# First mixture layer of a three-part kernel: its two projections fused per feature tile, against all features first with the gated product kept in DRAM

## The chip, the cores and the metric

The kernel runs on one core of one Trainium2 chip. The metric is the device time of one execution in microseconds (us), as the median of several runs. The engines are TensorE (PE for its matmuls, PEld for its weight loads), VectorE (DVE), ScalarE (ACT), GpSimd (POOL) and SyncE (SP), which issues every DMA here. PSUM has eight banks of 128 x 512 fp32, which matmuls write and DVE and ACT read.

## The reference

```python
q_s = softmax(q, over d);  k_s = softmax(k, over the sequence)      # 4 batches, 8 heads, 576 tokens, 64
attn = q_s @ (k_s^T @ v)                                            # linear attention
x = attn as 2304 tokens x 512
x = ((x @ w_a) * (x @ w_b)) @ w_out                                 # first layer: 512 -> 1536 -> 512
h = x @ w_in                                                        # second layer: 512 -> 2048
P = a0 + a1*h + a2*h^2 + a3*h^3
Q = 1 + |b0|*|h| + |b1|*h^2
out = (P / (Q + 1e-6)) @ w_out2                                     # 2048 -> 512
```

All five weight matrices reach the kernel as 64-bit floats. Each is turned into fp32 by integer arithmetic on the chip, and then, like every operand of a large matmul, parted into a high and a low part (hi + lo). A product of two such operands is three matmuls: hi x hi, hi x lo, lo x hi.

## The kernel before

Tokens lie along the free dimension. There are five token blocks: four wide ones of 512 and a narrow one of 256 (block 4). The first layer has 12 feature tiles of 128, and the hidden size 512 is four slices of 128. For one feature tile and one wide block, the input projection is 2 x 4 x 3 = 24 matmuls of 128x512 (`w_a` and `w_b`, four slices, three passes), and the output projection is 4 x 3 = 12.

Attention comes first: 16 units (batch, pair of heads), four to a batch. A unit loads kx, q, v (the last four also k), takes softmaxes on DVE, ACT and POOL, transposes on PE, and writes its slice of x into `XH` and `XL`. Token block 0 needs batch 0, block 1 needs batches 0 and 1, block 2 needs 1 and 2, blocks 3 and 4 need batch 3.

The first layer is fused per feature tile. For a feature tile f and a block n, `front` (or `raw_p`) projects into two banks, ACT copies the one, DVE multiplies the two in PSUM, and ACT and DVE part the product h into hi and lo in SBUF. Then its output projection is summed over some tiles in four banks and added to `ACC`, which holds the first layer's output in SBUF, four slices of 512 columns to a wide block:

- Tiles 0 to 2: `step1`, plain, for the blocks 0, 1, 2, 4, 3 in this order, between the attention units.
- Tiles 3 to 8, in three pairs, for two wide blocks at a time: the input projection is plain (`raw_p`), and the output projection is done by seven products in place of eight (`seven`, lines 604 to 640), a 2 x 2 block scheme after Strassen and Winograd with feature tiles on the one side and blocks on the other. The sums of h are made on DVE and POOL, the sums of the weights (`combined`) on POOL. A product is 3 matmuls here, twice (q = 0, 1): 2 x 7 x 3 = 42 matmuls where the plain form has 48. Block 4 is plain (`narrow_out`).
- Tiles 9 to 11: plain again (`step1`, and `late_jobs` for block 3).

Within one run of `seven` four banks are chained: bank bb starts as ACT's copy of bank ba, and DVE twice reads bb, adds s5 and writes another bank before PE may add the next product to bb.

Meanwhile the second layer's weights are converted, summed for its own seven-product scheme, parted and sent to DRAM (`spill_in` to `wi`, `spill_out` to `wo`). The second layer (`slot`, `value`, `jobs`) loads them back. Its input projection is by seven products for two feature tiles and two wide blocks, `value` computes the quotient P/Q on ACT, DVE and POOL, and `jobs` does the output projection.

The order on every engine is set by a list planner (class `Plan`). Each operation has an engine, an estimated duration and a rank. At every step the operation that can start earliest by the estimates is placed, and the rank breaks ties; the ranks come from the step number and from the table `K`. The result is one fixed order per engine, kept in the program. PE's gaps in the first 34 us of that plan are filled with 64 x 64 matmuls (line 1029) that compute nothing. DVE operations marked `port` and all POOL operations are planned so that they do not run at once.

Of the kernel before, what the change touches and what calls it, by code (L numbers as in the profile page):

```python
# [8 lines left out]
F32 = mybir.dt.float32  # L9
# [5 lines left out]
U32 = mybir.dt.uint32  # L15
# [15 lines left out]
class Plan:  # L31
# [4 lines left out]
    FILL_NS, FILL_MAX = 220, (99, 10)  # L36
    FILL_BEFORE, FILL_AFTER = 34000, 2000000
# [7 lines left out]
    def add(self, eng, ns, rank, fn, reads=(), writes=(), lat=0, port=False, kind=None):  # L45
# [13 lines left out]
        self.ops.append((eng, ns, rank, fn, deps, lat, port, kind))  # L59

    def run(self, fill=None):
# [15 lines left out]
        held, last = 0.0, None  # L77
        while any(pending.values()):
# [27 lines left out]
        for i in order:  # L106
            fill(-1 - i) if i < 0 else self.ops[i][3]()
# [3 lines left out]
def tile_kernel(ctx: ExitStack, tc: tile.TileContext, q, k, kx, v, w_a, w_b, w_out, w_in, w_out2, ca, cb, out):  # L111
# [23 lines left out]
    MID = [0, 1, 4, 2, 3]
    SC = 672
    HALF = W // 2
    OP = 2 * HALF
    SLOT = 2.5
    TURN1, NX, SW0, SW1, OP1 = 4, 2, 2, 3, NF2 // 2 - 1  # L140
    FREE, SEED = (4, 5, 6), (2, 3, 7)
    K = dict(late=-5.492, soon=-4.219, asoon=-10.236, wl=0.745, j0=0.985, j1=2.536, jn=-5.433, each=0.116, by=0.067, v1=1.075, v2=1.344, v3=2.483, v4=-0.278, v5=1.767, p1=0.009, px=-33.016, op=35.311, w2=-24.837, w2f=35.283, o0=-6.141, o1=0.018, l0=2.085, l1=1.554, l2=-8.695, l3=44.833, last=0.124, wd0=-177.696, wd1=-244.762, wd2=786.423, wd3=-216.948, wd4=-330.707, wd5=-371.667, wd6=-374.53, wd7=-318.414, wd8=945.62, wd9=-244.134, ud0=-407.821, ud1=-374.884, ud2=-251.536, ud3=774.452, ud4=866.463, ud5=897.008, ud6=902.77, ud7=-216.823, ud8=846.88, ud9=-177.926, ud10=868.092, ud11=818.136, ud12=-251.038, ud13=846.209, ud14=808.362, ud15=-311.04, wr0=-371.708, wr1=866.784, wr2=799.828, wr3=-388.518, wr4=858.306, wr5=-269.879, wr6=751.328, wr7=-450.468, wr8=887.219, wr9=846.842, ur0=-250.344, ur1=796.637, ur2=945.186, ur3=901.846, ur4=-216.266, ur5=723.759, ur6=856.445, ur7=-375.494, ur8=-270.336, ur9=709.668, ur10=-383.977, ur11=-376.01, ur12=-338.73, ur13=-335.107, ur14=945.651, ur15=-268.887, nx=7.017, wn=-21.267, sp=-2.053, se=2115.662, msoon=-6.362, madd=-62.481, mcomb=-16.671, mn=-103.581, mpe=0.747, mpb=0.526, mfr=-9.292, mw=-39.037)
# [14 lines left out]
    diag = const.tile([P, P], F32, name="diag")  # L157
    NW4 = NT // W * W
    SIDE = 16
    XH = const.tile([P, NCC, NW4], F32R, name="XH")  # L160
    XL = const.tile([P, NCC, NW4], F32R, name="XL")
    XN = const.tile([P, 8 * SIDE + 2 * NCC * (NT - NW4)], F32R, name="XN")

    def X(low, c, o, n):

        if o < NW4:
            assert o + n <= NW4
            return (XL if low else XH)[:, c, o:o + n]
        i = SIDE + (low * NCC + c) * (NT - NW4) + o - NW4
        return XN[:, i:i + n]  # L170

    def pieces(o, n):
        c = min(max(NW4 - o, 0), n)
        return [(a, b) for a, b in ((0, c), (c, n)) if b > a]

    ACC = const.tile([P, NCC * NT], F32, name="ACC")
    ps = [psum.tile([P, W], F32, name=f"ps{i}") for i in range(8)]
    Y, AB, AT = (0, 1, 2, 3), (4, 5), (6, 7)


# [13 lines left out]
    wa = Area((NW + NHL + NEW) * 2 * W, F32R, "wa")  # L194
    o_sc = NRAW * 2 * W
    o_g = o_sc + NSC * SC
    o_sg = o_g + 2 * W
    o_x = o_sg + 2 * W
    fa = Area(o_x + 2 * W, F32, "fa")

    small = tiles(2, [P, 8 * C5 + 3], F32, "small")
    mxs = tiles(2, [P, 1], F32, "mx")

    two = "p (a b) -> p a b"
    pair = lambda got: [(t.rearrange(two, a=2), k) for t, k in got]
# [18 lines left out]
    def pe(passes, n, rank, fn, reads, writes, fixed=3):  # L224
        plan.add("pe", passes * (n / 2.4 + fixed), rank, fn, reads, writes, kind="r" if passes == 3 else "f")
# [10 lines left out]
    def dve2(n, rank, fn, reads, writes):  # L236
        plan.add("dve", 65 + n * 0.85, rank, fn, reads, writes, port=True)
# [10 lines left out]
    def xk(name, c, o, n):  # L248
        return [(name, c, i) for i in range(o // 32, (o + n - 1) // 32 + 1)]
# [836 lines left out]
```

## Time and profile before

| | |
|---|---|
| median of 3 runs | 887.16 us (886.65 to 887.49) |
| profiled execution, from its first to its last instruction (span) | 885.0 us |
| what lies around the span, by the median | 2.16 us |
| TensorE busy | 875.9 us, 99% |
| weight loads busy | 727.4 us, 82% |
| DVE, ACT, POOL busy | 665.0, 572.6, 448.0 us |
| granted TensorE clock | 1.00, which is 2.4 GHz, over the whole span |
| DMA | 131.25 MB, 148 GB/s over the span |

The profile states no time of the profiled execution besides its span, so the span stands for it, and 2.16 us is added to get from spans to medians. A busy share near 100% on PE means that PE hardly ever waited. It does not say that each matmul ran at its peak, since consecutive matmuls overlap: their listed durations add up to more than the time between their starts. Times of PE work are therefore read from starts. The stages by the timeline: up to 24 us PE has only the attention's small matmuls; from 24 to about 140 us attention and first layer are mixed; the first layer alone runs until about 500 us, and the second until the end.

### The profile page before, as it was taken

To read this page: it belongs to the slowest core of one execution; us is meant where nothing else is said; L and a number is where in the kernel's file an instruction comes from. 1 tells how busy PE (TensorE), PEld (TensorE's weight loads), DVE (VectorE), ACT (ScalarE), POOL (GpSimd) and SP (SyncE) were. 2 spreads that over 40 slices of the span, in tenths; PEclk is the share of its full clock that TensorE was granted. 3 is DMA by queue.
4 is the path that set the end of the run, shared out by engine and by line. 5 is a ranking of instruction groups with operands and counts; after the bars stand their busy time and mean duration, and the time that the engine had idled before them with its cause. 6 is when DMAs were issued, how large, how long until landed. Compare 5 with 4: busy or idle time off the path is not lost.

```text
span 885.0 us, 13244 instructions
## 1 busy us (share of the span) xinstructions
PE 875.9 (99%) x4526; PEld 727.4 (82%) x4526; DVE 665.0 (75%) x1117; ACT 572.6 (65%) x1078; POOL 448.0 (51%) x421
## 2 busy tenths in 40 slices
PE   8999999999999999999999999999999999999998
PEld 7777778888888878888898888888888888888887
DVE  6887766657677675878665698779898878788883
ACT  6877566455455454454534598888888778887770
POOL 4654665355353545362536345455667644455541
PEclk9999999999999999999999999999999999999999
DMA  7866966524414343264542843352525364435222
GB/s 253 271 208 187 279 192 207 182 96 134 153 49 136 114 131 96 72 214 143 179 131 84 248 126 115 112 168 82 175 72 178 107 201 144 158 93 190 69 87 96
DMA packets 60180, 131.25 MB, mean 148 GB/s; under 512 B 6480, under 2 KB 14928, under 8 KB 60112
## 3 DMA queue, kind: packets, MB, share of 16 engines
q1 hardware_dynamic: 60112, 130.40, 46.1%
q8 instruction: 36, 0.59, 0.3%
q14 instruction: 32, 0.26, 0.1%
HBM read 100.49 MB, written 29.88 MB: 147 GB/s over the span
## 4 chain that ended last, share of the span: by engine, by line
PE 97%; DVE 1%; DMA 1%; ACT 0%; POOL 0%; issue 0%; SPq 0%; DVEq 0%; POOLq 0%
PE ps L522 23%; PE ps L524 22%; PE ps L523 22%; PE ps L800 6%; PE ps L802 6%; PE ps L801 6%; PE ps L622 2%; PE ps L624 2%; PE ps L623 2%; PE ps L499 2%; PE ps L464 1%; PE ps L489 1%; PE ps L442 1%; PE ps L1029 1%; DMA wa<-wo 1%; DMA ACC<-in_q 0%
## 5 line engine op out<-in xcount | busy, mean ns | idle before, releaser
L522 PE MATMUL ps<-wa 128*128 128x512 f32 (+1 forms) x428 | 163.2, 381 | 0.8 <-DMA wa<-wo 0.7
L524 PE MATMUL ps<-wa 128*128 128x512 f32 (+1 forms) x428 | 160.8, 376 | 0.0
L523 PE MATMUL ps<-wa 128*128 128x512 f32 (+1 forms) x428 | 160.7, 375 | 0.0
L522 PE MATMUL ps<-XH,wa 128*128 128x512 f32 x384 | 154.3, 402 | 0.0
L759 POOL TENSOR_TENSOR fa<-fa 128x512 f32<-128x512 f32 x72 | 93.4, 1300 | 115.8 <-ACT fa L757 99.5
L524 PE MATMUL ps<-XH,wa 128*128 128x512 f32 x384 | 150.0, 391 | 0.0
L523 PE MATMUL ps<-XL,wa 128*128 128x512 f32 x384 | 149.8, 390 | 0.0
L783 POOL TENSOR_TENSOR wa<-fa,wa 128x512 fp32r<-128x512 f32 x70 | 89.7, 1297 | 41.1 <-ACT wa L782 22.6
L540 DVE TENSOR_TENSOR ACC<-ps,ACC 128x512 f32<-128x512 f32 (+1 forms) x121 | 80.5, 679 | 31.3 <-PE ps L524 25.7
L522 PEld LDWEIGHTS ps<-wa 128*128 128x128 f32 x428 | 80.4, 188 | 17.4 <-DMA wa<-wo 1.1
L524 PEld LDWEIGHTS ps<-wa 128*128 128x128 f32 x428 | 80.4, 188 | 14.8
L523 PEld LDWEIGHTS ps<-wa 128*128 128x128 f32 x428 | 80.5, 188 | 14.4
L800 PE MATMUL ps<-XH,wa 128*128 128x512 f32 x224 | 87.3, 390 | 0.0
L802 PE MATMUL ps<-XH,wa 128*128 128x512 f32 x224 | 87.3, 390 | 0.0
L801 PE MATMUL ps<-XL,wa 128*128 128x512 f32 x224 | 87.2, 389 | 0.0
L524 PEld LDWEIGHTS ps<-XH,wa 128*128 128x128 f32 x384 | 72.1, 188 | 15.6
L522 PEld LDWEIGHTS ps<-XH,wa 128*128 128x128 f32 x384 | 72.2, 188 | 14.7
L523 PEld LDWEIGHTS ps<-XL,wa 128*128 128x128 f32 x384 | 72.2, 188 | 13.7
L349 POOL TENSOR_TENSOR fa<-fa 128x256 fp32r<-128x256 f32 x64 | 49.9, 794 | 55.9 <-ACT fa L348 44.0
L321 POOL TENSOR_TENSOR wa<-fa,wa 128x512 fp32r<-128x512 f32 x30 | 40.1, 1339 | 70.9 <-ACT wa L320 68.7
L766 DVE SCALAR_TENSOR_TENSOR fa<-fa,coef,ps 128x512 f32<-128x512 f32 x72 | 52.7, 741 | 16.2 <-ACT ps L765 15.9
L756 ACT ACTIVATE fa<-ps 128x512 f32<-128x512 f32 x72 | 42.5, 595 | 24.3 <-PE ps L802 11.0
(130 smaller groups left out, 1993.1 us busy)
## 6 DMA issues: line engine op xcount, KB each, us to landing
wa<-wi SPq DMA_DIRECT2D x120, 256.0 KB, 3.0
wa<-wo SPq DMA_DIRECT2D x32, 512.0 KB, 4.7
fa<-in_moe_w_out SPq DMA_DIRECT2D x28, 512.0 KB, 4.4
wi<-fa SPq DMA_DIRECT2D x40, 256.0 KB, 2.5
fa<-in_moe_w_in SPq DMA_DIRECT2D x16, 512.0 KB, 4.2
fa<-in_moe_w_b SPq DMA_DIRECT2D x12, 512.0 KB, 4.0
fa<-in_moe_w_a SPq DMA_DIRECT2D x12, 512.0 KB, 4.1
wi<-wa SPq DMA_DIRECT2D x24, 256.0 KB, 4.9
```

The costliest lines, as they stand in the source:

```text
L349: pool(HALF, rank, lambda: nc.gpsimd.tensor_tensor(out=lo, in0=src, in1=hi.bitcast(F32), op=ALU.subtract), [ksrc, kt], [kt])
L522: nc.tensor.matmul(o, lh, rh, start=start, stop=False)
L523: nc.tensor.matmul(o, lh, rl, start=False, stop=False)
L524: nc.tensor.matmul(o, ll, rh, start=False, stop=stop)
L540: dve(n, rank, lambda: nc.vector.tensor_tensor(out=a, in0=ps[bank][:, :n], in1=a, op=ALU.add), [psk(bank), ("accr", o)], [("accr", o)])
L756: act(n, rank, lambda: A.activation(u, h, AF.Abs), [kh], [ku])
L759: pool(n, rank, lambda: G.tensor_tensor(out=w, in0=w, in1=u, op=ALU.mult), [ku, kw], [kw])
L766: dve(n, rank, lambda: V.scalar_tensor_tensor(out=z, in0=z, scalar=coef[:, 0:1], in1=h, op0=ALU.add, op1=ALU.mult), [kz, kh], [kz], ptr=1)
L783: pool(W, rank, lambda: nc.gpsimd.tensor_tensor(out=hl[1], in0=z, in1=hl[0].bitcast(F32), op=ALU.subtract), [kz, kh], [kh])
L800: T.matmul(ps[bank], wh, xh, start=first, stop=False, skip_group_check=True)
L801: T.matmul(ps[bank], wh, xl, start=False, stop=False, skip_group_check=True)
L802: T.matmul(ps[bank], wl, xh, start=False, stop=last, skip_group_check=True)
```

## The change

The first layer is no longer fused. All 12 feature tiles are projected first, h goes to DRAM as fp32, and the output projection is a pass of its own.

- Tiles 0 to 2 are projected plainly (`plain`), tiles 3 to 11 by seven products (`strassen`) for the block pairs (0, 1) and (2, 3), with `w_a` and `w_b` of a tile as the two rows of the scheme and the two halves of the hidden size as its columns. Block 4 stays plain. One `strassen` is 7 x 2 x 3 = 42 matmuls for what took 48. The two block pairs use four banks each in turn.
- The sums of x that the scheme needs are made once for each block pair (`factors`), the sums of the weights for each tile (`product_weights`).
- `product` copies one bank on ACT, multiplies on DVE into SBUF, and `stored` sends the 128 x 512 fp32 result to DRAM (`h_d`, 60 tiles).
- `out1` then loads h back tile by tile (`loaded`, parted by ACT and DVE) and sums all 12 tiles in PSUM: first blocks 0 and 1 in all eight banks, then block 2, block 3, and block 4. The finished banks are copied by ACT; nothing is added to an SBUF sum.
- Weights are converted two tiles at a time (`converted`, 1024 columns an operation), and one of the integer steps moved from DVE to ACT for most of them. Parting and sums go to DVE or POOL in shares (`tt`).
- Spills of the second layer's weights have new places: eight during the seven-product phase, eight during `out1`.
- The attention's tiles rotate through three slots. Ranks of the whole plan, the second layer's too, are new (table `K`, left out here). The filler matmuls end at the first wide matmul.

The core of the difference:

```diff
+    def product(f, n, a, b, ka, kb, soon, rank):
+
+        nb = blocks[n][1]
+        gh, kg = r_gh.take()
+        gh, kg = gh[:, 0:nb], kg[:nb // GR]
+        act(nb, soon, lambda: A.activation(gh, a, AF.Copy), [ka], [kg])
+        dve(nb, soon, lambda: V.tensor_tensor(out=gh, in0=b, in1=gh, op=ALU.mult), [kb, kg], [kg])
+        stored(f, n, gh, kg, rank)
...
+        mult(ba, 0, True, False)
+        act(W, ranks(0) + soon, lambda: A.activation(ps[bb], ps[ba], AF.Copy), [psk(ba)], [psk(bb)])
+        mult(be, 1, True, True)
+        act(W, ranks(1) + soon, lambda: A.activation(s5, ps[be], AF.Copy), [psk(be)], [k5])
+        mult(ba, 2, False, True)
+        yield ba, 2
+        mult(bb, 3, False, True)
+        dve(W, ranks(3) + soon, lambda: V.tensor_tensor(out=ps[bc], in0=ps[bb], in1=s5, op=ALU.add),
+            [psk(bb), k5], [psk(bc)])
+        mult(bb, 4, False, True)
+        dve(W, ranks(4) + soon, lambda: V.tensor_tensor(out=ps[be], in0=ps[bb], in1=s5, op=ALU.add),
+            [psk(bb), k5], [psk(be)])
+        yield be, 4
+        mult(bc, 5, False, True)
+        yield bc, 5
+        mult(bb, 6, False, True)
+        yield bb, 6
...
+    for n in range(2):
+        jobs1 += [("pl", n, f) for f in range(M0)]
+    jobs1 += [("pl", 2, f) for f in range(M0)] + [("st", 0, M0)] + [("pl", 3, f) for f in range(M0)]
+    jobs1 += [("pl", NB - 1, f) for f in range(M0)] + [("st", 1, M0), ("pl", NB - 1, M0)]
+    for f in range(M0 + 1, NF1):
+        jobs1 += [("st", 0, f), ("st", 1, f), ("pl", NB - 1, f)]
...
-    def step1(f, n, banks, start, stop, first, final, rank):
-        hh, ll, kh = front(f, n, banks, rank)
...
-    def raw_p(i, f, n, banks, rank):
...
+    def loaded(f, n, at):
+
+        nb = blocks[n][1]
+        t, kt = r_hl.take()
+        h, l = (t[:, 0:nb], kt[:nb // GR]), (t[:, nb:2 * nb], kt[nb // GR:2 * nb // GR])
+        x, kx_ = r_h.take()
+        x, kx_ = x[:, 0:nb], kx_[:nb // GR]
+        dma(P * nb * 4, at - K["hdlead"], lambda: nc.sync.dma_start(out=x, in_=h_d[f][n]), [("h", f, n)], [kx_])
+        split((x, kx_), (h, l), at, SH[2])
+        return h, l
+
+    def out1(ns, banks, us):
...
```

The order shows it at three places. First SP's queue at the very start of the program, before and then after; each row is one DMA, `in_kx`, `in_q`, `in_v` are one attention unit's inputs.

```order
L430 DMA fa<-in_kx 128x576
L430 DMA ACC<-in_q 128x640
L430 DMA fa<-in_v 128x650
L430 DMA fa<-in_kx 128x576
L430 DMA ACC<-in_q 128x640
```

```order
L404 DMA fa<-in_moe_w_b 128x1024
L309 DMA fa<-in_kx 128x576
L309 DMA fa<-in_q 128x640
L309 DMA fa<-in_v 128x650
L309 DMA fa<-in_kx 128x576
L309 DMA fa<-in_q 128x640
L309 DMA fa<-in_v 128x650
L404 DMA fa<-in_moe_w_a 128x1024
L404 DMA fa<-in_moe_w_b 128x1024 x2
```

A weight tile of 512 KB now stands ahead of the first unit's loads, and three more ahead of the third unit's.

Second, PE in one run of seven products, in the first layer, with the engines that a row waits for in brackets. Before (banks `ps_75` and `ps_76` belong to `seven`, `ps_79` to an input projection):

```order
L624 MATMUL ps_75<-wa 128x512
L622 MATMUL ps_76<-wa 128x512 [waits Activation_49]
L623 MATMUL ps_76<-wa 128x512 [waits Pool_49]
L624 MATMUL ps_76<-wa 128x512
L522 MATMUL ps_79<-XH,wa 128x512
L523 MATMUL ps_79<-XL,wa 128x512
L524 MATMUL ps_79<-XH,wa 128x512
L622 MATMUL ps_75<-wa 128x512 [waits Activation_49]
```

And after (`ps_79` is bank bb, `ps_77` is ba, `ps_80` is bc; six matmuls of a product follow each other):

```order
L543 MATMUL ps_77<-wa 128x512
L541 MATMUL ps_79<-wa 128x512 [waits DVE_49]
L542 MATMUL ps_79<-wa 128x512
L543 MATMUL ps_79<-wa 128x512 [waits Pool_49]
...
L543 MATMUL ps_80<-wa 128x512
L541 MATMUL ps_79<-wa 128x512 [waits DVE_49]
L542 MATMUL ps_79<-wa 128x512
```

Before, matmuls of an input projection stand between the dependent products; after, only the products of the same run do.

Third, DVE in the same stage after the change, between the two adds of one run (L596 and L599; L424 is a step of a weight conversion, L436 a sum for it, L563 the gated product).

```order
L421 TENSOR_SCALAR fa<-fa 128x1024
L596 TENSOR_TENSOR ps_80<-ps_79,fa 128x512
L424 SCALAR_TENSOR_TENSOR fa<-fa 128x1024
L436 TENSOR_TENSOR fa<-fa 128x256 x2
L599 TENSOR_TENSOR ps_78<-ps_79,fa 128x512
L419 SCALAR_TENSOR_TENSOR fa<-fa 128x1024
L563 TENSOR_TENSOR fa<-ps_78,fa 128x512
```

A conversion step of 1024 columns and up to two sums stand between the adds on which PE waits.

## Rows read from the trace of the kernel before

**Rows 1.** The page: span, busy time by engine, and the chain that ended last.

```profile
span 885.0 us, 13244 instructions
...
PE 875.9 (99%) x4526; PEld 727.4 (82%) x4526; DVE 665.0 (75%) x1117; ACT 572.6 (65%) x1078; POOL 448.0 (51%) x421
...
PE 97%; DVE 1%; DMA 1%; ACT 0%; POOL 0%; issue 0%; SPq 0%; DVEq 0%; POOLq 0%
```

**Rows 2.** Busy time by stage; after the engines granted clock, DMA share, GB/s.

```profile
0.00:24.00 24.00, 20.65 (x229) 17.10 (x229) 17.15 (x37) 16.19 (x37) 10.44 (x14) 1.00 0.78 259
24.00:75.00 51.00, 51.00 (x338) 38.51 (x337) 44.55 (x88) 40.56 (x93) 28.51 (x23) 1.00 0.70 222
75.00:150.00 75.00, 75.00 (x469) 58.91 (x469) 55.29 (x110) 48.19 (x115) 41.60 (x47) 1.00 0.75 231
150.00:500.00 350.00, 348.63 (x1719) 294.79 (x1718) 241.13 (x417) 168.27 (x336) 168.31 (x184) 1.00 0.40 131
500.00:850.00 350.00, 349.30 (x1631) 292.29 (x1630) 287.47 (x436) 288.39 (x481) 188.11 (x148) 1.00 0.43 134
```

**Rows 3.** PE's waits after the start: total us, times, longest.

```profile
PE ps L622 <- DVE ACC L540: 1.3, 2, 0.9
PE ps L522 <- DMA wa<-wo: 0.7, 1, 0.7
```

**Rows 4.** PE by shape: input projection, and first pass of `seven`.

```profile
L522 PE MATMUL ps<-XH,wa 128*128 128x512 f32 x384 | 154.3, 402 | 0.0
L622 PE MATMUL ps<-wa 128*128 128x512 f32 x84 | 33.5, 399 | 1.4 <-DVE ACC L540 1.3
```

**Rows 5.** PE timeline in the last jobs: start, duration; between them 30 wide matmuls.

```profile
868.10 0.39 PE L523 MATMUL ps<-wa 128*128 128x512 f32 x1
875.12 0.39 PE L524 MATMUL ps<-wa 128*128 128x512 f32 x1
```

**Rows 6.** Timeline of the start: SP's first and third kx, PE's first transposes, first projection.

```profile
0.74 0.38 SPq L430 DMA_DIRECT2D fa<-in_kx  x1
6.38 0.33 SPq L430 DMA_DIRECT2D fa<-in_kx  x1
5.51 0.76 PE L442 MATMUL ps<-ident,fa 128*128 128x128 f32 x5
23.93 0.50 PE L522 MATMUL ps<-XH,wa 128*128 128x512 f32 x1
```

**Rows 7.** Groups by shape on DVE and ACT: busy us, mean ns.

```profile
L634 DVE TENSOR_TENSOR ps<-ps,fa 128x512 f32<-128x512 f32 x12 | 8.3, 695 | 6.4 <-PE ps L624 6.3
L311 DVE SCALAR_TENSOR_TENSOR fa<-fa 128x512 int32<-128x512 int32 x65 | 49.4, 769 | 0.0
L730 DVE TENSOR_TENSOR ACC<-ACC 128x512 f32<-128x512 f32 x16 | 11.1, 701 | 0.0
L727 DVE TENSOR_TENSOR XL<-ACC,XH 128x512 fp32r<-128x512 f32 x11 | 10.4, 954 | 3.5 <-ACT XH L723 3.5
L629 ACT ACTIVATE ps<-ps 128x512 f32<-128x512 f32 x12 | 7.0, 584 | 13.0 <-PE ps L624 7.3 <-DVE ACC L540 5.7
L306 DVE TENSOR_SCALAR fa<-fa 128x512 int32<-128x512 int32 x65 | 30.1, 476 | 5.1 <-DMA fa<-in_moe_w_b 3.0 <-DMA fa<-in_moe_w_a 1.7 <-DMA fa<-in_moe_w_in 0.4
```

**Rows 8.** Timeline around PE's longest wait in `seven`.

```profile
317.25 2.71 POOL L580 TENSOR_TENSOR wa<-fa,wa 128x512 fp32r<-128x512 f32 x2 [1.63 <-ACT wa L575]
317.30 1.54 DVE L306 TENSOR_SCALAR fa<-fa 128x512 int32<-128x512 int32 x1
318.75 0.68 DVE L540 TENSOR_TENSOR ACC<-ps,ACC 128x512 f32<-128x512 f32 x1
319.49 0.50 PE L622 MATMUL ps<-wa 128*128 128x512 f32 x1 [0.92 <-DVE ACC L540]
```

**Rows 9.** DMA issues: count, KB each, median us from issue to landing.

```profile
wi<-wa SPq DMA_DIRECT2D x24, 256.0 KB, 4.9
out<-ACC SPq DMA_DIRECT2D x17, 256.0 KB, 2.1
```

More of the change, by code (lines that the diff above doesn't have):

```diff
@@ L157, in tile_kernel @@
     diag = const.tile([P, P], F32, name="diag")
+    small = tiles(2, [P, 8 * C5 + 3], F32, "small")
+    mxs = tiles(2, [P, 1], F32, "mx")
     NW4 = NT // W * W
     SIDE = 16
[L160 to L178, printed above, removed]
     GR = 32
@@ new lines, in tile_kernel, with spilled @@
+    PROD = ("A11", "S1", "A12", "S2", "S3", "S4", "A22")
+    NAMES = ("A11", "A12", "S1", "S2", "S3", "S4", "A21", "A22")
+    NP1, NP2 = NF1 // 2, NF2 // 2
+    wi_d = [dram.tile([P, 8 * OP], F32, name=f"wi{j}") for j in range(NP2)]
+    w2_d = [dram.tile([P, 2 * W], F32, name=f"wo{f}") for f in range(NF2)]
+    h_d = [[dram.tile([P, nb], F32, name=f"h{f}_{n}") for n, (t0, nb) in enumerate(blocks)]
+           for f in range(NF1)]
+    def spilled(x, kx_, n, rank, out, kout, share=0.0):
+        t, kt = r_st.take()
+        parted(by(x, n), kx_, cells(t.bitcast(F32R), n), kt, rank, share)
+        dma(P * 2 * W * 4, rank + K["std"], lambda: nc.sync.dma_start(out=out, in_=t), [kt], kout)
@@ new lines, in plain, with seven, mult @@
+    def plain(f, n, banks, rank):
+        t0, nb = blocks[n]
+        ba, bb = banks
+        soon = rank + K["fsoon"]
+        proj("a", f, n, ba, rank)
+        proj("b", f, n, bb, rank, nb if ba == bb else 0)
+        pa = ps[ba][:, 0:nb]
+        pb = ps[bb][:, nb:2 * nb] if ba == bb else ps[bb][:, 0:nb]
+        product(f, n, pa, pb, psk(ba), psk(bb), soon, rank)
+    def seven(banks, products, ranks, soon):
+        ba, be, bb, bc = banks
+        s5, k5 = r_s5.take()
+        def mult(bank, i, start, stop):
+            terms = products(i)
+            for j, (wh, wl, xh, xl, keys) in enumerate(terms):
+                first, last = start and j == 0, stop and j == len(terms) - 1
+                pe(3, W, ranks(i), lambda wh=wh, wl=wl, xh=xh, xl=xl, first=first, last=last: mm3(
+                    ps[bank], wh, wl, xh, xl, first, last), keys + ([] if first else [psk(bank)]), [psk(bank)])
+        mult(ba, 0, True, False)
[15 more added lines that the diff above has]
+        yield bb, 6
@@ new lines, in tile_kernel, with spill @@
+    end1 = us
+    first_use = {}
+    for (kind, n, f), t in zip(jobs1, when):
+        first_use.setdefault(f, t)
+    spill1 = [('i', 0), ('2', 0), ('i', 1), ('2', 2), ('i', 2), ('2', 4), ('i', 3), ('2', 6), ('i', 4), ('i', 5), ('2', 8), ('i', 6), ('2', 10), ('i', 7), ('2', 12), ('2', 14)]
+    for u in range(NPAIR):
+        attention(u, K[f"ur{u}"], K[f"ud{u}"])
+    nspill = [0]
+    def spill(many, rank):
+        for _ in range(many):
+            kind, f = spill1.pop(0)
+            r = rank + K[f"sp{nspill[0]}"]
+            (spill_i if kind == "i" else spill_2)(f, r, r - K["dlead"])
+            nspill[0] += 1
```

861 lines of the change are left out of this document (384 added, 477 removed).

## The prediction

> **What bounds the kernel now.** I read the page first: PE is busy 99% of an 885.0 us span, and 97% of the chain that ended last is PE [rows 1]. A high busy share can hide waiting, so the stages come next [rows 2]: PE is busy 51.00 of 51.00 and 75.00 of 75.00 us while attention and first layer are mixed, 348.63 of 350 in the first layer alone, 349.30 of 350 in the second. The list of waits agrees: after the start PE waits 1.3 us for DVE inside `seven` and 0.7 us for a weight DMA [rows 3]. The granted clock is 1.00 (2.4 GHz) in every stage. So after 24 us the time is the number of matmuls times their pitch. The listed durations are no pitch (402 ns for a 128x512 matmul [rows 4]), because neighbours overlap. The pitch is read from starts: 868.10 to 875.12 us holds 31 steps [rows 5], 7.02 / 31 = 0.2265 us.
>
> The other engines matter only where they could make PE wait. From 24 to 75 us DVE is busy 44.55 of 51 (87%) and ACT 40.56 (80%); in the second layer both are at 82%, and PE still loses only 0.7 us of 350 [rows 2].
>
> **Part 1, the matmuls.** Count 128x512 matmuls of the first layer for the wide blocks. Before: input 12 tiles x 4 blocks x 24 = 1152 (the row shows 384 first passes, times three [rows 4]); output plain for 6 tiles, 6 x 4 x 12 = 288; output by seven for 3 pairs x 2 block pairs, 84 each, 252 (84 first passes, times three [rows 4]). Sum 1692. After: input 3 x 4 x 24 = 288 plain and 9 x 2 x 42 = 756 by seven; output 12 x 4 x 12 = 576. Sum 1620. The input projection gets 108 cheaper and the output 36 dearer. Block 4, attention and the second layer keep their counts. 72 x 0.2265 = 16.3 us less, all of it on the path.
>
> The Trainium skill ("TensorE: Matmul & The Clock Gate", "Wait — 56ns, not 53.3ns?") gives 215.7 ns from start to start for 512 columns. The trace has 226.5 here, so the measurement is used; by the page the saving would be 15.5 us.
>
> **Part 2, the start.** The first unit's kx was issued at 0.74 us and its transposes ran at 5.51 [rows 6]. Now 512 KB of `w_b` go ahead of it. At the 259 GB/s of this stage [rows 2] that is 2.0 us. The third unit's loads have three more weights (5.9 us of traffic) ahead of them; but before they had to wait for a buffer until 6.38 us [rows 6]. Against this, nine wide matmuls now stand before the third unit's last product where three stood, so PE has something to do. Bounds: 0 and 6 us; I take 1, near the 2.0 of the first load less the work put in front.
>
> **Part 3, attention.** PE now has less other work to spread between the units: 24 matmuls for a tile and block instead of 36. By the two orders, 102 wide matmuls stood ahead of the ninth unit's product and now 72; ahead of the twelfth 159 and 114; ahead of the last 312 and 288. For PE never to wait, the twelfth unit must be done 45 x 0.2265 = 10.2 us sooner and the last 5.4 us sooner. What helps is that DVE loses work here: no parting of h, no sums into `ACC`, no conversion of `w_out`. Adding rows of the forms in [rows 7] along both orders, I get ahead of the twelfth unit about 80 us of DVE work before and 69 after, of ACT 80 and 73. ACT is the tight one: at its 80% [rows 2] the 7 us save 7 / 0.80 = 9 us where PE comes 10.2 sooner. Ahead of the ninth unit ACT has about 60 us before and 59 after, so it saves 1.3 us where PE comes 30 x 0.2265 = 6.8 us sooner. Bounds: 0 (DVE was the limit and is relieved) and 6 us (ACT keeps its share, and the ninth unit is 5.5 us late). I take 2, since ACT has idle time to give up.
>
> **Part 4, seven products back to back.** 18 runs, each with two adds on DVE (36 in all) that PE needs. Between the product that an add reads and the next one into the same bank lies one other product, 6 x 0.2265 = 1.36 us. The add takes 0.695 us [rows 7]; about 0.6 us are left for DVE to get there. ACT's copy (0.584) has as much. DVE's load here, per tile of 21.7 us of PE (84 matmuls, and block 4's 24 of half the width at half the pitch): seven products 4 x 0.70, gated products 4 x 0.70 + 0.4, two conversions with three steps each of 1024 columns (two at twice 0.769 at most, one at twice 0.476, so 4.0 each), half the sums and partings, 5 at most: about 19 us, 88%. The second layer at 82% cost PE 0.7 us [rows 2], but there jobs fill in. In the old `seven`, with projections between its products, 12 runs cost 1.3 us [rows 3]. Scaled to 18 that is 2.0. Bounds: 0, and 36 x 0.92 = 33 us if each add comes as late as the worst one of before [rows 3]. I take 2, nearest the row of the same chain, and 1.3 go away with the old one.
>
> What made the worst wait is in the trace: a `TENSOR_SCALAR` on DVE, 0.476 us on average [rows 7], took 1.54 us because it started 0.05 us after a POOL operation, the add behind it came late, and PE waited 0.92 us [rows 8]. The Trainium skill ("SBUF — State Buffer", "Who interferes with whom") says that a DVE operation of this kind, or one with two SBUF inputs, and a GpSimd operation lock each other out for a whole instruction. The trace agrees with it in this one place. The rule speaks against the change, because its sums run on DVE and POOL in turn; what it would do is the first rival.
>
> **Part 5, h through DRAM.** 48 stores of 256 KB and 12 of 128 KB, and as many loads: 28 MB more. They lie in stages at 0.40 DMA share [rows 2]. A load lands 2.1 to 4.9 us after its issue [rows 9], one is needed every 2.72 us of PE (12 matmuls), and five buffers let them run ahead 13 us; ACT and DVE need about 1.4 us to part one. So the loads hide; if not, each of the 48 pays. In `out1` DVE has the partings, six conversions of `w_out` and four spills in 65 us: at 0.701 a sum about 52 us, at 0.954 [rows 7] about 61. Changes of bank set cost something at the end of each block group, and `wo`'s 0.7 us may come or go. Bounds -0.7 and 5 us; I take 1.
>
> **The sum.** -16.3 + 1 + 2 + 2 - 1.3 + 1 = -11.6 us against the profiled 885.0, so a span of 873.4; with 2.16 us around it, 875.6. The largest added terms lean to their upper guesses: parts 2 and 3 overlap, since a unit that starts late and an engine that is late are the same wait. I count 1.5 less and predict **874**.
>
> **Rivals.**
> 1. *The seven-product chain stalls PE, and it is slower.* Place: the two DVE adds of each of 18 runs. Price: 36 times the lateness; slower than before from 15.1 / 36 = 0.42 us each on (the saving without part 4 being 16.3 + 1.3 - 1 - 2 - 1 + 1.5 = 15.1). With 0.7 us each it is 887.2 - 15.1 + 25.2 = 897. For it: [rows 8], 1024-column steps between the adds, and nothing of another job between the products. Against it: two late ones in 12 runs, and PE at 99.8% in the second layer with DVE at 82%. Chance 0.08.
> 2. *The attention gets too thin a cover.* PE waits for ACT, DVE or the loads of the first 100 us: parts 2 and 3 at their upper ends without overlap, 12 us in place of the 1.5 that the forecast leaves them: 874 + 10.5 = 884; less gain, or hardly any. For it: ACT's share near 90%, weights ahead of the units' loads. Against it: 11 us less DVE work. Chance 0.12.
> 3. *The loads of h come late*, because SP's queue issues in order and stands behind stores and spills that wait: 48 x 0.3 = 14 us, 887, no change. For it: SP has half as many DMAs again. Against it: five buffers. Chance 0.05.
> 4. *Nothing new shows*, only the matmuls and the old waits go: 887.16 - 16.3 - 2.0 = 869. Chance 0.12.
>
> **How the numbers follow.** My forecast, 870 to 880 as its own range, has 0.63. No change, within 0.2% (about what a measurement here can tell), is 885.4 to 888.9: the top of rival 2 and rival 3, 0.05. Slower: rival 1, and a little of 2 and 3, 0.08. Faster: 0.87. The range is 868 to 883: it takes in rival 4 and most of rival 2, and leaves out rival 1, rival 3 and the top of 2, some 0.18.
>
> **What would show it.** Part 1: 1620 wide first-layer matmuls at the same pitch, at a clock of 1.00; if the pitch or the clock falls the sum falls with it. Part 2: first transposes near 7.5 us, first wide matmul within 2 us of 23.93. Part 3: PE waits for ACT-made or POOL-made tiles before about 90 us, together 1 to 4 us. Part 4: waits of PE on L596 and L599, 1 to 4 us over all 18 runs; 10 or more would be rival 1. Part 5: no PE wait on the parting of `h` beyond 1 us at a time, and a few tenths at the changes of bank set. I am wrong if PE's idle time after 24 us exceeds 10 us.

## The result, and the profile of the changed kernel

The changed kernel takes 876.96 us (median of 4 runs, 875.71 to 878.36), the kernel before beside it 887.01 us (4 runs): a ratio of 0.9883, 95% interval 0.9869 to 0.9897. It is 10.1 us faster. The forecast was 874.0 us, 13 us faster, with a range of 868 to 883 us.

The page first, as in [rows 1]: the span, busy time and share by engine with the number of instructions, and the chain that ended last.

```profile
span 874.9 us, 12881 instructions
...
PE 859.9 (98%) x4448; PEld 714.3 (82%) x4448; DVE 662.2 (76%) x984; ACT 600.3 (69%) x1028; POOL 391.1 (45%) x317
...
PE 93%; DMA 3%; DVE 2%; ACT 1%; issue 1%; POOL 0%; SPq 0%; POOLq 0%; ACTq 0%
```

The span fell by 10.1 us. PE's busy time fell by 16.0, and its idle time (span less busy) rose from 9.1 to 15.0 us. So the saving is there, and 5.9 us of it went into waiting. The stages say where; the columns are those of [rows 2].

```profile
0.00:24.00 24.00, 19.66 (x200) 16.65 (x200) 16.61 (x35) 14.29 (x33) 10.76 (x14) 1.00 0.75 251
24.00:75.00 51.00, 48.51 (x364) 36.56 (x365) 40.34 (x85) 41.49 (x99) 39.70 (x31) 1.00 0.76 242
75.00:150.00 75.00, 73.60 (x429) 57.02 (x428) 51.77 (x83) 37.37 (x76) 39.84 (x32) 1.00 0.44 150
150.00:500.00 350.00, 349.35 (x1714) 295.31 (x1713) 251.45 (x328) 213.93 (x332) 102.83 (x84) 1.00 0.66 229
500.00:850.00 350.00, 347.08 (x1644) 290.53 (x1643) 295.20 (x446) 292.38 (x491) 193.34 (x153) 1.00 0.41 132
```

PE's idle time, before and after: 3.35 and 4.34 us up to 24 us; 0 and 2.49; 0 and 1.40; 1.37 and 0.65; 0.70 and 2.92; behind 850 us 3.7 and 3.2. The differences are +1.0, +2.5, +1.4, -0.7, +2.2 and -0.5, together +5.9. The stage that was rebuilt lost less than before. The losses lie at the start, in attention, and in the second layer, whose arithmetic is the same and whose order is not.

PE's waits, as in [rows 3] (total us, times, longest):

```profile
PE ps L368 <- POOL fa L356: 2.3, 2, 1.4
PE ps L541 <- DVE ps L900: 1.9, 1, 1.9
...
PE ps L378 <- ACT fa L370: 1.1, 1, 1.1
PE ps L541 <- DMA wa<-wo: 1.0, 1, 1.0
PE ps L378 <- ACT fa L315: 0.9, 1, 0.9
PE ps L368 <- DVE kvbd L359: 0.7, 1, 0.7
PE ps L543 <- POOL wa L438: 0.7, 1, 0.7
PE ps L329 <- DVE wa L392: 0.5, 1, 0.5
PE ps L541 <- ACT ps L895: 0.5, 1, 0.5
PE ps L343 <- ACT fa L325: 0.3, 1, 0.3
```

L596 and L599, the additions of the seven products, are not in the list, nor is the parting of `h` (L640). The list leaves out waits under 0.15 us.

### The profile page after: what moved, and what is told of

The parts are those of the page before. It is cut to its first block, busy times and chain, and to the rows that moved or that the text cites. A ratio compares the mean times of both kernels' runs of the same rounds, so it can differ in the third digit from the quotient of the medians.

```text
span 874.9 us, 12881 instructions
## 1 busy us (share of the span) xinstructions
PE 859.9 (98%) x4448; PEld 714.3 (82%) x4448; DVE 662.2 (76%) x984; ACT 600.3 (69%) x1028; POOL 391.1 (45%) x317
## 4 chain that ended last, share of the span: by engine, by line
PE 93%; DMA 3%; DVE 2%; ACT 1%; issue 1%; POOL 0%; SPq 0%; POOLq 0%; ACTq 0%
PE ps L541 30%; PE ps L543 29%; PE ps L542 29%; PE ps L378 2%; DMA fa<-in_q 1%; PE ps L343 1%; PE ps L368 1%; DMA fa<-in_kx 1%; DMA wa<-wo 1%; DMA fa<-in_moe_w_b 1%; PE ps L321 1%; SPq L404 0%; DVE small L347 0%; ACT fa L839 0%; DVE fa L436 0%
## 5 line engine op out<-in xcount | busy, mean ns | idle before, releaser
L541 PE MATMUL ps<-wa 128*128 128x512 f32 (+1 forms) x1264 | 475.5, 376 | 3.6 <-DVE ps L900 1.9
L543 PE MATMUL ps<-wa 128*128 128x512 f32 (+1 forms) x1264 | 469.1, 371 | 0.7 <-POOL wa L438 0.7
L542 PE MATMUL ps<-wa 128*128 128x512 f32 (+1 forms) x1264 | 468.6, 371 | 0.0
L541 PEld LDWEIGHTS ps<-wa 128*128 128x128 f32 x1264 | 237.6, 188 | 48.4 <-DVE ps L900 2.1
L543 PEld LDWEIGHTS ps<-wa 128*128 128x128 f32 x1264 | 237.5, 188 | 43.1 <-POOL wa L438 1.3
L542 PEld LDWEIGHTS ps<-wa 128*128 128x128 f32 x1264 | 237.6, 188 | 39.8
L438 POOL TENSOR_TENSOR fa<-fa 128x256 f32<-128x256 f32 (+2 forms) x66 | 73.6, 1124 | 169.8 <-ACT fa L444 80.9
L438 POOL TENSOR_TENSOR wa<-fa,wa 128x512 fp32r<-128x512 f32 x41 | 56.3, 1376 | 96.4 <-ACT wa L444 72.0
L436 DVE TENSOR_TENSOR wa<-fa,wa 128x512 fp32r<-128x512 f32 (+1 forms) x89 | 69.6, 790 | 27.1 <-ACT wa L640 20.4
L640 ACT ACTIVATE wa<-fa 128x512 fp32r<-128x512 f32 (+1 forms) x76 | 44.3, 596 | 47.3 <-PE ps L543 26.7
L847 DVE SCALAR_TENSOR_TENSOR fa<-fa,coef,ps 128x512 f32<-128x512 f32 x72 | 52.2, 742 | 13.2 <-ACT ps L846 13.0
L841 DVE TENSOR_TENSOR fa<-fa,ps 128x512 f32<-128x512 f32 x72 | 48.4, 681 | 15.1 <-ACT fa L839 15.0
L838 ACT ACTIVATE fa<-fa,bmag 128x512 f32<-128x512 f32 x72 | 57.5, 810 | 0.0
L839 ACT ACTIVATE fa<-ps,coef 128x512 f32<-128x512 f32 x72 | 55.6, 774 | 2.2 <-PE ps L543 1.8
L436 DVE TENSOR_TENSOR fa<-fa 128x256 f32<-128x256 f32 (+2 forms) x66 | 47.6, 741 | 9.8 <-ACT fa L444 8.0
L842 DVE SCALAR_TENSOR_TENSOR fa<-fa,coef,ps 128x512 f32<-128x512 f32 x72 | 52.5, 744 | 0.9
L849 DVE SCALAR_TENSOR_TENSOR ps<-fa,qbias,ps 128x512 f32<-128x512 f32 x72 | 52.6, 749 | 0.0
```

Source lines behind the costliest of these rows:

```text
L436: dve(n, rank, lambda: V.tensor_tensor(out=o[0], in0=x[0], in1=y[0], op=op), [x[1], y[1]], [o[1]], port=True)
L438: pool(n, rank, lambda: G.tensor_tensor(out=o[0], in0=x[0], in1=y[0], op=op), [x[1], y[1]], [o[1]])
L541: T.matmul(o, lh, rh, start=start, stop=False, skip_group_check=True)
L542: T.matmul(o, lh, rl, start=False, stop=False, skip_group_check=True)
L543: T.matmul(o, ll, rh, start=False, stop=stop, skip_group_check=True)
L838: act(n, rank, lambda: A.activation(w, u, AF.Identity, scale=bmag[:, 1:2], bias=bmag[:, 0:1]), [ku], [kw], ptr=2)
```

## Experiments

The experiments ran in four sets. The kernel before ran beside each and took 886.6 to 887.3 us by its median. The changed kernel was measured with the result and again in the first set, 2.6 us apart, so smaller differences between sets tell little.

**The changed kernel again.** In the first set it ran once more, as the yardstick for the kernels beside it.

> The changed kernel once more, as the yardstick for the three kernels beside it. Expected: 877.0 +-1.2 us, a ratio of 0.987 to 0.990 to the kernel before, and the same places of PE waits: about 3.2 us at 23.9, 27.4 and 30.2 us, 0.7 at 86 us, 0.5 at 499 us, 1.9 at 512.6 us, 1.0 at 774 us. If these waits move between executions, they are not the program's order but chance.

Measured: 879.53 us (877.75 to 880.75, 5 runs), ratio 0.9902 (0.9889 to 0.9916). The larger waits came at the same places. The 0.96 us for `wo` at 774 us did not come, and two of 0.7 us were new (for L392 at 50.35 and for `wi` at 489.83 us), so by the expectation these are chance and not the program's order. Besides, this profile has a stretch at half clock behind the wait of 1.85 us in the second layer. Below are PE's matmuls there (start, duration), and then busy time and granted clock (the figure behind the last bracket) in steps of 2 us.

```profile
514.51 0.59 PE L541 MATMUL ps<-wa 128*128 128x512 f32 x1 [1.85 <-DVE ps L900]
...
516.18 0.63 PE L542 MATMUL ps<-wa 128*128 128x512 f32 x1
516.61 0.63 PE L543 MATMUL ps<-wa 128*128 128x512 f32 x1
...
518.50 0.40 PE L542 MATMUL ps<-wa 128*128 128x512 f32 x1
```

```profile
514.00:516.00 2.00, 1.49 (x4) 1.20 (x5) 1.97 (x4) 2.00 (x5) 1.60 (x2) 0.69 0.70 285
516.00:518.00 2.00, 2.00 (x6) 1.52 (x6) 1.83 (x3) 1.77 (x5) 2.00 (x4) 0.50 0.12 47
518.00:520.00 2.00, 2.00 (x10) 1.65 (x9) 0.84 (x2) 1.47 (x5) 1.46 (x3) 0.95 0.71 125
```

The pitch is 0.43 us there instead of 0.23: the lower level, 1.2 GHz. What it cost is 2 x (0.31 + 0.50 + 0.05) = 1.7 us. In the first profile the same wait (1.85 us, at 512.64) was followed by a clock of 1.00. So one program has two outcomes, about 1.7 us apart by this estimate. That does not explain the 2.6 us between its two medians: by the mean clock of each run, 0.995 went with 877.19 us beside the result and 0.998 with 878.56 and 879.78 us here. What separates the two medians stays open.

**Part 1: 72 matmuls put back.**

```
-    mm3(ps[bank], wh, wl, xh, xl, first, last)
+    [T.matmul(ps[bank], wh, xh, start=True, stop=False) for _ in range(2 * first)] + [mm3(...)]
```

> In each of the first layer's eighteen jobs by seven products the first matmul of the products that open a bank (two per job) is sent three times instead of once: it overwrites what it wrote, so the result is the same, and 72 wide matmuls are back, the number that the change took away, with nothing else moved. Theory (part 1: PE is the bound, each wide matmul is worth its pitch of 0.2265 us): 16.3 us more than the changed kernel (877 to 880 us), so 893 to 896 us, and PE's busy time 16.3 us up. Rival (the stage with the seven products is bound by the sums, copies and transfers around it, so that the gain came from elsewhere): under 8 us more, and idle time of PE falls instead.

Measured: 895.57 us, 18.6 and 16.0 us above the two medians of the changed kernel. In the profile (clock 1.00) the span is 18.5 us up: PE's busy time is 876.9 us, 17.0 up, where 72 x 0.2265 = 16.3 were expected, and 1.5 us are more waiting. Theory holds: 72 matmuls are worth what was counted for them, and nothing else in that stage hides them.

**Part 4: each addition of the seven products twice.**

```
-    V.tensor_tensor(out=ps[bc], in0=ps[bb], in1=s5, op=ALU.add)
+    [V.tensor_tensor(out=ps[bc], in0=ps[bb], in1=s5, op=ALU.add) for _ in range(2)]    # and ps[be]
```

> Each of the 36 bank-to-bank additions of the first layer's seven products (VectorE, L596 and L599, 0.70 us) is sent twice; the second writes the same values. Theory (part 4 cost nothing because each addition is covered by exactly one other product of 6 matmuls, 1.36 us: read from the changed kernel, the addition at 241.21 us ends at 241.91 and its bank is written again at 242.30, a slack of 0.4 us): the second addition of about 0.6 us passes the slack by 0.2 to 0.35 us with the matmul's restart, 36 times: 7 to 13 us more, PE waits on L596 and L599 up from 0 to that sum. Rival (the cover is wider, PE has other ready work to take in between): no waits on these lines and under 2 us more.

Measured: 895.34 us; the span is 892.8, 17.9 up. The mechanism is the theory's: waits on L596 and L599 went from 0 to 7.5 us in 29 instances. The price was not: 15.8 and 18.4 us above the two medians. One place, PE and DVE (start, duration; x2 are two additions):

```profile
238.13 1.43 DVE L599 TENSOR_TENSOR ps<-ps,fa 128x512 f32<-128x512 f32 x2
...
238.99 0.39 PE L543 MATMUL ps<-wa 128*128 128x512 f32 x1
239.61 0.50 PE L541 MATMUL ps<-wa 128*128 128x512 f32 x1 [0.23 <-DVE ps L599]
239.94 0.39 PE L542 MATMUL ps<-wa 128*128 128x512 f32 x1
```

The list calls this a wait of 0.23 us. By starts, 238.99 to 239.94 is 0.95 us for two steps that take 0.453 without a wait: 0.50 us are lost, and 36 x 0.50 = 18; the same reading at the 34 places that can be paired between the two traces gives 17.8 us. A listed wait costs about 0.27 us more than its figure here, since the matmuls no longer overlap. The same additions single, in the changed kernel, end 0.39 to 0.53 us before the bank is needed at 33 of these 34 places. At the other, 171.01 us, PE waited 0.11 us for L596, too short for the list, and lost 0.39 us by starts. So part 4 was free by a margin of about 0.4 us at all places but one.

**Part 5: the loads of `h`.** First each load was issued twice.

```
-    nc.sync.dma_start(out=x, in_=h_d[f][n])
+    [nc.sync.dma_start(out=x, in_=h_d[f][n]) for _ in range(2)]
```

> Each of the 60 loads of h from DRAM is issued twice, the second writing the same values into the same tile: 14.2 MB more through the queue in the first output projection, and each tile ready one transfer later. Theory (part 5 cost nothing since five tiles of h are in flight and one tile feeds PE for 12 matmuls, 2.7 us, so that a load of 3.0 us has about 10 us): PE waits in the output projection stay under 2 us and the time within 2 us of the changed kernel. Rival 3 of the prediction (the loads come just in time): 60 times 1 to 3 us, 30 us or more, with PE waiting for L640 and L438.

Measured: 989.59 us, over 110 us more. This is no test of the loads' lead: the second load writes the tile of the first, so it waits for its landing, and SyncE's queue stands meanwhile. This is SyncE's own list of waits:

```profile
SPq L744 <- DMA fa<-h: 185.5, 62, 5.7
```

What it does show is the price of waiting DMAs in SyncE's queue: everything behind them is late. A lower clock is in the 110 us too (0.95 on average). The second try adds the traffic without the wait.

```
+    nc.sync.dma_start(out=dram.tile([P, nb], F32), in_=h_d[f][n])     # ahead of each load of h
```

> Ahead of each of the 60 loads of h, a copy of the same tile from DRAM to another place in DRAM is issued, which nobody waits for: 14.2 MB more through the queue, none of them into SBUF, and SyncE has one issue of 0.3 us more before each load. Unlike the doubled loads (989.6 us, where the second load waited in SyncE's queue for the landing of the first) nothing is made to wait. Theory (part 5: the loads of h are far enough ahead, five tiles in flight): no PE wait over 2 us in the output projection, and the time within 2 us of the changed kernel, 876 to 881 us. Rival (the loads come just in time, so any lengthening shows): each load later by its copy's 1 to 3 us, PE waits on L640 and L438, and 10 us or more in time.

Measured: 880.73 us (ratio 0.9930, 0.9914 to 0.9947). PE lost 0.94 us between 200 and 475 us, where the changed kernel loses nothing; 0.7 of it is listed on L640. With 14.2 MB more in the queue the loads begin to show, so their lead is real and not large. Theory holds at its edge.

**Second layer: three instructions set ahead.** In this kernel and those of the start, a few instructions are moved in one engine's queue after the planner has run; the rest of the queues stays. Here VectorE's queue at the wait of 512.6 us, where `ps_79` is the bank that PE waits for (- is the place in the changed kernel, + the new one):

```
-L841 TENSOR_TENSOR fa<-fa,ps_83
 L849 SCALAR_TENSOR_TENSOR ps_79<-fa,qbias,ps_79
-L847 SCALAR_TENSOR_TENSOR fa<-fa,coef,ps_82
 L851 SCALAR_TENSOR_TENSOR fa<-ps_79,fa
-L849 SCALAR_TENSOR_TENSOR ps_82<-fa,qbias,ps_82
 L900 TENSOR_TENSOR ps_79<-ps_80,fa
+L841 TENSOR_TENSOR fa<-fa,ps_83
+L847 SCALAR_TENSOR_TENSOR fa<-fa,coef,ps_82
+L849 SCALAR_TENSOR_TENSOR ps_82<-fa,qbias,ps_82
```

> Second layer, third unit of work: three VectorE instructions (L849, L851, L900) are set ahead of three others (L841, L847, L849 of another chain); nothing else moves. Theory (the wait at 512.6 us, 1.85 us, is a matter of place in VectorE's queue: the bank that L900 writes is freed by L851, and two steps of other chains of 0.6 us each stand before each of them; PE is the bound, so what it does not wait is gained in full): the wait falls from 1.85 to under 0.3 us and the time by 1.5 to 1.9 us. Rival (the three delayed instructions feed PE's next work, so the wait comes back within 20 us): the wait at 512.6 goes, another of 1 to 2 us appears before 535 us, time within 0.4 us of the changed kernel.

Measured: 875.90 us (875.07 to 877.71), ratio 0.9867 (0.9850 to 0.9884): 3.6 us under the yardstick beside it, more than expected, and the lowest median of the study. These are PE's waits of that kind in its profile, and the clock at the place:

```profile
PE ps L541 <- DVE ps L902: 0.5, 1, 0.5
...
PE ps L541 <- DVE ps L900: 0.3, 1, 0.3
```

```profile
512.00:514.00 2.00, 1.90 (x10) 1.25 (x8) 1.97 (x4) 2.00 (x5) 1.62 (x3) 1.00 0.91 347
514.00:516.00 2.00, 2.00 (x9) 1.57 (x9) 1.97 (x4) 2.00 (x5) 2.00 (x4) 1.00 0.93 305
```

The 1.85 us became 0.3, 0.5 came back at the next addition (the rival, in part), and the fall of the clock went with the wait: 1.05 + 1.7 = 2.8 of the 3.5 us between the two profiled spans. Against the first profile, which had no fall, the span is only 0.6 us shorter, and against the result's ratio (0.9883, 0.9869 to 0.9897) the intervals overlap. So it is shown that the wait is a matter of place in VectorE's queue; the gain by the medians is 1.1 or 3.6 us, by which run of the changed kernel it is set against. Of the profiles with the wait whole (L900, 1.8 to 1.9 us; the doubled loads of `h` left aside) the clock fell behind it in four, the yardstick and three experiments (0.97 over 475 to 525 us), and stayed at 1.00 in three. In the five kernels with the new order it was 1.00 over that stretch in all.

The Trainium skill ("TensorE: Matmul & The Clock Gate", "🔬 Part 1: The HAM clock gate (the "warmup" mystery)") says that the gate follows how busy TensorE has lately been and does not run in step with the kernel, so that the same kernel can differ from run to run. The four and three profiles with the same wait agree with it.

**The start, six times.** First ACT's byte step behind two copies that PE waits for, and the third pair's softmax ahead of a weight's steps:

```
 ACT:  L415 behind L370, L373;  L350 ahead of L388       POOL: L356 ahead of L348
 DVE:  L347 ahead of L419;  L351, L354, L355 ahead of L424
```

> Start: the byte step of a weight (ACT L415, which waits 1.49 us for its DMA) is set behind L370 and L373, and the softmax chain of the third pair (ACT L350, DVE L351 to L355, POOL L356) is set ahead of a weight's steps and of the fourth pair's subtraction. Theory (the waits of PE at 27.4 us, 1.38, and 30.2 us, 1.11, come from such places in the queues of ACT and POOL, not from there being fewer wide matmuls beside attention): both fall under 0.5 us, and the time by 1.5 to 2.5 us. Rival (there is too little wide work ahead, as the prediction's third part had it: whichever instruction is put first, another one is late): the waits move to other lines between 24 and 60 us, sum still over 2.5 us, time within 0.5 us of the changed kernel.

Measured: 879.30 us, as the yardstick and, in time, as the rival has it. PE's idle time from 24 to 75 us was 1.68 us, where the yardstick had 3.24. PE's L378 came at 28.92 instead of 30.24 us, and then the clock fell to 0.50 (1.2 GHz) until about 33 us, which costs 2 x (0.25 + 0.50 + 0.10) = 1.7 us. The wait for POOL's L356 fell from 1.38 to 0.31 us, and one of 0.99 for POOL's L438 appeared. The next kernel moved the 512 KB of the first weight behind two pairs' loads, with the weight's steps:

```
 SP:  kx, q, v, kx, q, v, moe_w_b, moe_w_a, ...      instead of   moe_w_b, kx, q, v, kx, q, v, moe_w_a, ...
```

> Start: the 512 KB of the first weight are loaded behind the first two pairs' keys, queries and values instead of ahead of them, and the weight's own steps on ACT, DVE and POOL stand correspondingly later. Theory (the second part of the prediction: 512 KB take 2.0 us of the loads' stream, and the first pair's chain sets when the wide work begins): first transposes at 5.6 to 6.1 us instead of 7.75, and the time falls by 1 to 2 us. Rival (the wide work begins when the weight is split, and that now comes later): the first transposes are as early, but the first wide matmuls wait for POOL or ACT of the weight, and the time is the same within 0.5 us or up to 2 us longer.

Measured: 887.43 us (885.51 to 888.43), 8 us slower: neither expectation. SyncE issued nothing between 4.72 and 19.50 us:

```profile
4.01 0.71 SPq L404 DMA_DIRECT2D fa<-in_moe_w_a  x1
19.50 0.80 SPq L404 DMA_DIRECT2D fa<-in_moe_w_b  x2
```

There the third weight's load waits for the first weight, whose buffer it takes (5.5 us for its landing, 9.2 for its split on POOL), and the third pair's loads stand behind it. PE then waited 5.75 us for VectorE's L359, until 27.62 us, and its clock was 0.50 from 24 to 30 us; how much of the 8 us is the clock was not separated. In the changed kernel the same load waits from 5.3 to 11.0. So the next one set the third pair's loads ahead of it, on top of the order of the second layer:

```
 SP:  ..., moe_w_a, q, v, kx, moe_w_b, moe_w_b, ...    instead of   ..., moe_w_a, moe_w_b, moe_w_b, kx, q, v, ...
```

> The three VectorE instructions of the second layer set ahead as in the kernel before it (time then 875.9 us), and besides, in SyncE's queue, the loads of the third pair (query, value, keys) ahead of the third weight's load, which at 4.7 to 11.0 us waits for its buffer (freed by POOL L438) and holds them up until 12.8 us. Theory (the first wide stretch is late because of that place in SyncE's queue: VectorE's L314 of the third pair waits for keys until 18.9 us, and L359 of the second pair, which PE's L378 needs, stands behind it): L314 of the third pair starts before 16 us, PE's L378 at about 19.5 instead of 20.7 us, and 1 to 2 us less: 874 to 875 us. Rival (the start is a chain with nothing spare, and the clock granted to PE falls when it has little to do there): what is gained comes back as other waits or as a stretch at half clock before 50 us; 875.5 to 877.5 us.

Measured: 877.10 us, ratio 0.9878 (0.9858 to 0.9899), no gain over 875.90. Its PE was 1.5 us ahead at 28.70 and then lost it; L314 stood at 17.92, and VectorE was not idle just before it: steps of a weight stand ahead of it in VectorE's own order.

```profile
28.70 2.29 PE L378 MATMUL ps<-fa,kvbd 128*128 128x288 f32 x4 [0.57 <-ACT fa L370]
```

```profile
26.00:28.00 2.00, 1.62 (x8) 1.04 (x8) 0.94 (x3) 1.04 (x3) 2.00 (x3) 1.00 1.00 354
28.00:30.00 2.00, 1.43 (x4) 1.01 (x4) 1.75 (x3) 0.76 (x3) 1.08 (x2) 0.62 0.89 289
30.00:32.00 2.00, 2.00 (x10) 1.56 (x8) 0.69 (x1) 1.37 (x3) 1.03 (x1) 0.53 0.69 263
```

Here 2 x (0.38 + 0.47) = 1.7 us went to the lower clock, after PE had waited 0.67, 1.38 and 0.57 us. But the clock is not the whole of it: two of the four executions had a mean clock of 1.000 and took 876.55 and 877.08 us, the two with 0.998 took 877.13 and 877.44. In the profile PE also waited 1.8 us for `wo` in the second layer, 0.4 in the kernel with VectorE's order alone. Two more kernels filled those gaps with small matmuls that add zero to a bank in use.

```
+    T.matmul(ps[3][0:64, 0:64], ident[0:64, 0:64], diag[0:64, 64:128], start=False, stop=True)
```

> The kernel with the three VectorE instructions and the third pair's loads set ahead (877.1 us, its PE at half clock for about 3 us from 28.5 us on), and besides: one more ACT instruction of the second layer ahead (L895 before the table load), and 11 small matmuls that add zero, put into PE's queue at the three places where it waits between 22 and 30 us. Theory (the load order gained 1.0 to 1.5 us by 28 us and the clock took it back: PE had little to do between 22 and 28 us): with the gaps filled the granted clock stays at 1.00 between 24 and 34 us, and the time is 873.5 to 875 us. Rival (the fall of the clock does not hang on what stands in these gaps, or matmuls by zeros do not count for it): half clock again at 28 to 32 us, time 876.5 to 878 us.

> As the kernel before it, and in addition the moves at the start (the byte step behind L370 and L373, the third pair's softmax chain ahead), with 9 small matmuls that add zero where PE then waits. Theory: the moves at the start brought PE's L378 from 30.24 to 28.92 us before the clock fell; with the clock held and the earlier loads it comes at about 27.5 us, and the time is 872 to 874 us. Rival (what is set ahead makes the weight's split late: POOL L438, 0.99 us in the kernel with these moves): 874 to 877 us, no better than without these moves.

Measured: 877.53 us, in the rival's range, and 879.91 us, above both. In the first the clock fell all the same (0.53 and 0.62 from 30 to 34 us), and L378 at 20.95 us waited 1.45 again, behind the third pair's L315 on ACT. In the second it stayed at 1.00, but PE waited 1.59 at 21.16 us, and 1.34 at 34.09 us for L383. So filling did not hold the clock in the first, and where the clock held, the kernel was no faster. Each order of the start brought another instruction late. The move of L895 did the same: its 0.53 us went, and PE waited 1.0 us for L851 in both kernels. The last one tested the 512 KB once more, with SyncE's queue mended:

> The kernel with the three VectorE instructions and the third pair's loads set ahead (877.1 us; its first transposes at 7.3 us, its PE L378 of the second pair at 19.7 us), and now the first weight's 512 KB behind the first pair's keys, queries and values, its steps on DVE, ACT and POOL behind that pair's, and 9 of the 31 small matmuls that fill PE's time before the first transposes left out. In the earlier kernel that moved the 512 KB, the third weight's load held SyncE's queue from 4.7 to 19.5 us; here the third pair's loads stand ahead of it. Theory (second part of the prediction: 512 KB ahead of the first keys are 2.0 us of the start): first transposes at 5.3 to 6 us, PE's L378 of the first pair at 12 to 13 instead of 14.7 us, and 1 to 2 us less in time: 875 to 876 us. Rival (the wide work begins with the second pair and the weights, whose bytes come no earlier): the first pair is 2 us earlier, PE's first L541 at 21.6 us as before or later, time 876.5 to 879 us.

Measured: 881.87 us, above both ranges. Beside the kernel that it is built on, the first transposes came at 6.08 us instead of 7.50, but the first pair's L378 at 16.18 instead of 14.67, behind waits of 2.22 us for POOL and 1.48 for ACT, and PE's first L541 at 26.14 instead of 21.62. The third weight's load was issued at 16.14 instead of 10.86, again waiting for the first weight's buffer, and the granted clock was 0.79 from 8 to 24 us, with some of the filling matmuls left out. Earlier transposes do not bring the wide work earlier, as the rival says; that the first pair would then be 2 us earlier, it had wrong.

## Why the prediction came out as it did

The direction and the range were right, and so was the main term: PE is the bound, and 72 wide matmuls are worth their pitch. The first pass is now one line of 1048 128x512 matmuls where [rows 4] and its companions had 1072, so 3 x 24 = 72 are gone. Busy time fell by 16.2 us besides 0.2 more of fill, and putting 72 back cost what they saved. The other terms had the wrong sizes, with errors of both signs. That the time came within 3 us of the forecast is in part luck, since they offset each other:

- **Part 2 and 3, start and attention: +1.5 net forecast, +4.9 measured** (1.0 + 2.5 + 1.4). Up to 24 us it is +1.0, as part 2 has it; the other 3.9 stand where part 3 had +2 and 1.5 were taken off. The signs named came true: transposes at 7.75 us, first wide matmul at 22.62, waits of 3.9 us for ACT, POOL and DVE between 23 and 90 us. But the 1.5 us taken off for overlap was unfounded, and the reason given was not the one. ACT was to be the tight engine, and 1.11 of the 3.9 us are for it; 2.05 are for POOL, which part 3 does not count and whose busy time rose from 28.51 to 39.70 of 51 us between 24 and 75 us. The chain that ended last goes through the loads (start, us, what):

```profile
1.65 5.47 DMA fa<-in_q
...
9.68 1.31 POOL wa L438
11.38 1.31 SPq L404
12.79 6.11 DMA fa<-in_kx
18.92 0.77 DVE mx L314
...
23.89 5.13 DMA fa<-in_moe_w_b
...
79.61 4.59 DMA fa<-in_q
```

  The third unit's loads are late for their place in SyncE's queue, behind a weight that waits for its buffer: its kx is issued at 12.79 us, where it was 6.38 [rows 6]. Set ahead, they did not shorten the time (877.10 us), so this is where the chain runs and not a cause shown. The 512 KB in front do hold up the first transposes by 2.2 us, near the 2.0 worked out, but that is not what the kernel loses: with them behind, it was 8 us slower than the yardstick and 5 us slower than the kernel it was built on. In both, the third weight's load came later, since the first weight's split frees its buffer, and the clock fell. That part 3 would come from fewer wide matmuls beside attention was not tested by itself: the start moves shifted the waits and did not lower the time, which fits it and does not prove it.
- **Part 4: +2 forecast, 0.1 of waiting measured** (0.4 by starts, at 171.01 us), and the old 1.3 us went as said. The additions take 0.700 and 0.698 us, as in [rows 7]. The step that was too high is DVE's load: 88% worked out, 217.40 of 300 us (72%) measured from 175 to 475 us, and DVE stood idle for PE before 17 of the 18 L596. A conversion takes 3.26 us where 4.0 was put, so two are 1.5 us of the about 3.4 that a tile needs less; the steps of double width take less than twice the row of single width (mean ns behind the bar):

```profile
L419 DVE SCALAR_TENSOR_TENSOR fa<-fa 128x1024 int32<-128x1024 int32 x31 | 38.9, 1255 | 5.2 <-ACT fa L415 5.2
L424 DVE SCALAR_TENSOR_TENSOR fa<-fa 128x1024 int32<-128x1024 int32 x31 | 38.8, 1252 | 4.1 <-ACT fa L423 4.1
L421 DVE TENSOR_SCALAR fa<-fa 128x1024 f32<-128x1024 f32 x31 | 23.4, 756 | 0.7
```

  The collision of [rows 8] between a DVE and a POOL instruction is not seen to delay an addition; POOL is busy 29% in that stretch. The doubled additions show how near it was.
- **Part 5: +1 forecast, 0 measured** in the output projection; a load of `h` lands in 3.0 us and PE waits for none. (The 2.1 to 4.9 us that the prediction reads as loads are stores in [rows 9].)
- **The second layer, not in the sum: +2.7** (2.2 behind 500 us, L895's 0.5 just ahead). The prediction priced only what the diff moves in the first layer. The table of ranks also reorders the second one, and two waits came there (L900 1.85, L895 0.53), in every profile of that order; `wo` went from 0.7 to 0.96, and was absent in the second profile. This is the term that was missing. The experiment shows for L900 that the order is the cause; L895's wait went too when it was set ahead, but one of 1.0 us came for it.

Against the span of 871.9 us that the sum with its 1.5 off gives, the errors are +0.3 (part 1), +3.4, -2.0, -1.0 and +2.7, and -0.5 at the end of the kernel: +2.9 of the +3.0 measured (874.9). The line drawn at 10 us of idle time after 24 us was crossed: it was 10.7. By the prediction's own sign its account of the waits was wrong. But the line was drawn badly too, for the kernel before had 5.7 by the same count, 3.7 of them behind 850 us.

## What to carry to other kernels

In a kernel bound by PE, count matmuls times their pitch first; that term held to 0.3 us. Then look at every stage whose order the change touches, also one whose instructions are the same, and ask of each engine's queue, SyncE's above all, what stands behind an instruction that waits. A short wait of PE can cost more than its figure, 0.50 us for a listed 0.23 here.

## What the hardware showed that was not expected

- A wait of PE listed as 0.23 us cost 0.50 us from start to start; with 36 such places the span grew by 17.9 us.
- One wait of 1.85 us was followed by a stretch at 1.2 GHz in four profiles and not in three; by the granted clock such a stretch cost 1.7 us, there and at the start (0.62 and 0.53 granted, 28 to 32 us). Executions with and without it are not that far apart in time: 877.13 and 877.44 us at a mean clock of 0.998, 876.55 and 877.08 at 1.000.
- A second DMA into the tile of a first one held SyncE's queue 3.0 us at a time, 185.5 us in all, and the kernel took 110 us longer, at a mean clock of 0.95.
